# Three x tiles loaded early and transposed on TensorE instead of two, with K by chunk of wk and then Q tile by tile, in a gated mix of linear attention and a feed-forward block

## The chip, the cores and the metric

The kernel runs on one core of one Trainium2 chip. The metric is device time in microseconds (us). Before the change it is 274.4 us, the median of three runs (274.22 to 274.67). The record gives their granted TensorE clock as 1.0 over the whole span; that figure does not count a start at half rate. Names used below: PE is the TensorE matmul, PEld its weight load, DVE is VectorE, ACT is ScalarE, SP is SyncE. SP and ACT each issue DMAs into a queue of their own.

## The reference

Only the head of branch A matters here: x (2048 x 640) times the K, Q and V parts of `wqkv`, and a gate per row.

```python
def _A_ref(x, wqkv, wo):
    qkv = ...(x @ wqkv)...                       # H = 32 heads of 20
    phi = lambda t: jnp.where(t > 0, t + 1, jnp.exp(t)) + 1e-6
    pq, pk = phi(q), phi(k)
    ...                                          # linear attention, then @ wo
g = _sigmoid((x * gate_w).sum(-1, keepdims=True))
return g * a + (1 - g) * b                       # b: a GEGLU feed-forward block on x
```

## The kernel before

x is cut into 16 tiles of 128 rows, and its 640 columns into 5 chunks. For each tile the kernel computes K and Q (phi of both is kept). A matmul needs x transposed. Tiles 0 and 1 are loaded as they are and transposed on TensorE (`T`); tiles 2 to 15 are transposed by the DMA. K of tiles 0 and 1 runs chunk by chunk while the chunks of wk land. The gate's logit comes out of the Q matmul as a 129th column: `gate_col` transposes `gate_w` on PE into a column of wq.

The loads, in their order in the program (SP is the queue unless "act" is given):

```python
load touch ("act"); load_x(0); load_wk(0)
load_x(1, "act")
load_wk(1); load_wk(3)
... exp table load on ACT ...
load_wk(2, "act"); load_wk(4, "act")
P.op("dve", lambda e: e.memset(gw_sb, 0.0), writes=[r_gw])
dma_in(gw_sb[0:5, :], gate_w.rearrange("(k p) -> k p", p=128), [r_gw], eng="act")
load_wq(0, 2); load_wq(2, KC, "act")
for i in range(NXN, NT):                         # NXN = 2: DMA transposes on SP, after wk4
    load_xT(i, after=([r_wk[4]] if i == NXN else ()))
... x again for later, then the feed-forward weights ...
```

The order on PE. `KM(n, ks)` adds chunks `ks` into the K of item n, one matmul of 512 columns and one of 128 per chunk; `QM` does it for Q. An item n owns the pair of PSUM banks `SLOTS[n % 4]`. `phi1` is the exp on ACT, `phi2` two operations on DVE; only after them is the pair of banks free.

```python
seq = [("k", 0), ("k", 1), ("q", 0), ("q", 1)]
warm(5, 512); warm(1, 128)                       # matmuls of constants, to keep PE busy
T(0, [0], 7); T(0, [1, 2, 3, 4], 6); warm(6, 128)
KM(0, [0])
T(1, [0], 7); T(1, [1, 2, 3, 4], 6); warm(3, 128)
KM(1, [0])
for k in (1, 3): KM(0, [k]); KM(1, [k])
gate_col()
for k in (2, 4): KM(0, [k]); KM(1, [k])
for n in range(4):
    if n == 2: ...                               # Q of tiles 0 and 1, chunks interleaved
    phi1(n); phi2(n)
for i in range(2, NT):
    KQ(i)                                        # K and Q of a tile together, 15 matmuls
```

## Time and profile before

| | before |
|---|---|
| time, median of the first 3 runs | 274.4 us |
| span of the profiled run | 273.2 us, PE busy 269.7 us |
| first K matmul | 4.62 us |
| gate column | 7.56 us |
| first Q matmul | 8.67 us |
| tile 2 (first joint tile) starts | 11.40 us |

First the page of the kernel before: its span line, PE's busy time (us, share of the span, instructions), and the chain that ended last, by engine and by line.

```profile
span 273.2 us, 3449 instructions
PE 269.7 (99%) x1369; PEld 128.6 (47%) x1369; DVE 141.9 (52%) x251; ACT 76.0 (28%) x132; POOL 30.0 (11%) x28
...
PE 97%; DMA 2%; SPq 0%; DVE 0%; issue 0%
PE ps L701 41%; PE ps L865 23%; PE ps L540 14%; PE ps L597 6%; PE ps L844 4%; DMA pool<-in_A_wqkv_dram 2%; PE ps L679 2%; PE ps L812 2%; PE ps L600 1%; PE ps L468 1%; PE ps L825 1%; PE ps L453 1%; PE ps L722 1%; PE ps L740 0%; SPq L340 0%; PE ps L469 0%
```

PE makes up the chain but for 2% spent on one load of wqkv. Next, PE's waits in the first 60 us of the kernel before: who waited for whom, us in total, how often, the longest.

```profile
PE ps L419 <- PEq L915: 0.8, 1, 0.8
PE ps L453 <- DMA pool<-in_A_wqkv_dram: 0.8, 2, 0.6
```

So PE waits for the program to start, and twice for wk, and never again. The timeline of PE (start, duration, line, tiles, shape; what ended an idle time stands in brackets) shows where. L453 and L454 are the two matmuls of `KM`, L498 is the gate column, L468 begins Q, L540 is `KQ`.

```profile
6.20 0.22 PE L454 MATMUL ps<-pool 128*128 128x128 bf16 x1
7.01 0.39 PE L453 MATMUL ps<-pool 128*128 128x512 bf16 x1 [0.59 <-DMA pool<-in_A_wqkv_dram]
...
7.56 0.17 PE L498 MATMUL ps<-pool 128*128 128x5 bf16 x1
...
8.67 0.38 PE L468 MATMUL ps<-pool 128*128 128x512 bf16 x1
...
11.40 5.79 PE L540 MATMUL ps<-pool 128*128 128x512 bf16 x31
```

A matmul's drawn end lies behind its true occupation of PE, so starts are the better measure: a pair of 512 and 128 columns starts 0.27 us after the last one, and here 0.81 us pass between 6.20 and 7.01 where 0.06 would do. That is a hole of 0.75 us, ended by wk3. It is what the change goes after.

### The profile page before, as it was taken

What the parts mean: (1) busy time and instruction counts of PE and PEld (TensorE: products, weight loads), DVE (VectorE), ACT (ScalarE), POOL (GpSimd) and SP (SyncE); (2) the same over time, 40 slices, a digit from 0 to 9 for tenths busy, and PEclk for the clock granted to TensorE, in tenths of its full rate; (3) what the DMA queues carried; (4) which work ended last, traced back from release to release, by engine and by line L of the source; (5) the groups of instructions that cost most, each with busy time, mean ns of one, the idle gap of its engine ahead of it and who ended that gap; (6) DMA issues with size and microseconds to landing.
All of it is one profiled execution on the core that took longest, in us unless ns stands there. A gap on an engine that the chain in (4) does not pass through costs nothing.

```text
span 273.2 us, 3449 instructions
## 1 busy us (share of the span) xinstructions
PE 269.7 (99%) x1369; PEld 128.6 (47%) x1369; DVE 141.9 (52%) x251; ACT 76.0 (28%) x132; POOL 30.0 (11%) x28
## 2 busy tenths in 40 slices
PE   7999999999999999999999999999999999999997
PEld 4555555544445444444444444444444444444444
DVE  2588989998234334999999999634210000000200
ACT  2355555310421454223222223224011121121021
POOL 5000000003240001242332422000000000000000
PEclk9999999999999999999999999999999999999999
DMA  6675999500300011522121221263031110110211
GB/s 207 179 118 122 322 402 386 143 3 12 65 19 2 23 49 51 182 45 48 26 48 24 48 42 34 60 215 109 5 77 38 41 38 19 38 41 19 58 58 41
DMA packets 42160, 23.61 MB, mean 86 GB/s; under 512 B 31519, under 2 KB 40735, under 8 KB 42015
## 3 DMA queue, kind: packets, MB, share of 16 engines
q1 hardware_dynamic: 41269, 22.40, 30.0%
q10 hardware_dynamic: 874, 0.98, 1.0%
q8 instruction: 11, 0.18, 0.3%
q14 instruction: 6, 0.05, 0.0%
HBM read 13.83 MB, written 2.63 MB: 60 GB/s over the span
## 4 chain that ended last, share of the span: by engine, by line
PE 97%; DMA 2%; SPq 0%; DVE 0%; issue 0%
PE ps L701 41%; PE ps L865 23%; PE ps L540 14%; PE ps L597 6%; PE ps L844 4%; DMA pool<-in_A_wqkv_dram 2%; PE ps L679 2%; PE ps L812 2%; PE ps L600 1%; PE ps L468 1%; PE ps L825 1%; PE ps L453 1%; PE ps L722 1%; PE ps L740 0%; SPq L340 0%; PE ps L469 0%
## 5 line engine op out<-in xcount | busy, mean ns | idle before, releaser
L701 PE MATMUL ps<-pool 128*128 128x512 bf16 x520 | 113.7, 379 | 0.0
L701 PEld LDWEIGHTS ps<-pool 128*128 128x128 bf16 x520 | 50.5, 98 | 60.0
L865 PE MATMUL ps<-pool 128*128 128x512 bf16 (+2 forms) x306 | 62.7, 367 | 0.0
L707 ACT ACTIVATE pool<-ps 128x512 f32<-128x512 f32 x52 | 31.0, 597 | 73.1 <-PE ps L701 73.1
L709 DVE TENSOR_TENSOR pool<-ps,pool 128x512 bf16<-128x512 f32 x52 | 34.7, 689 | 31.7 <-PE ps L701 30.4
L865 PEld LDWEIGHTS ps<-pool 128*128 128x128 bf16 x306 | 29.2, 98 | 33.4 <-issue 0.4
L540 PE MATMUL ps<-pool 128*128 128x512 bf16 (+1 forms) x210 | 38.1, 344 | 0.0
L848 DVE TENSOR_TENSOR pool<-ps,pool 128x512 bf16<-128x512 f32 x4 | 2.8, 692 | 61.5 <-PE ps L844 61.5
L755 POOL TENSOR_TENSOR pool<-pool 128x640 f32<-128x640 bf16 x16 | 22.5, 1406 | 72.9 <-DVE pool L757 66.2
L872 ACT ACTIVATE pool<-ps,pool 128x512 bf16<-128x512 f32 (+1 forms) x16 | 10.9, 681 | 68.6 <-PE ps L865 68.6
L540 PEld LDWEIGHTS ps<-pool 128*128 128x128 bf16 x210 | 20.5, 98 | 17.5
L559 DVE SCALAR_TENSOR_TENSOR pool<-ps,pool 128x128 bf16<-128x128 f32 (+2 forms) x42 | 25.3, 602 | 2.4
L550 ACT ACTIVATE pool<-ps 128x640 bf16<-128x640 f32 x28 | 19.7, 704 | 18.2 <-DVE pool L559 10.9
L597 PE MATMUL ps<-pool 128*128 128x512 bf16 x78 | 19.4, 379 | 0.0
L765 DVE TENSOR_TENSOR pool<-pool 128x640 bf16<-128x640 bf16 x16 | 13.2, 826 | 0.6
L763 DVE TENSOR_SCALAR pool<-pool 128x32 f32<-128x32 f32 x16 | 12.8, 802 | 0.6
L757 DVE TENSOR_REDUCE pool<-pool 128x32 f32<-128x640 f32 x16 | 12.9, 807 | 0.0
L645 DVE TENSOR_TENSOR pool<-pool 128x640 f32<-128x640 f32 x14 | 11.6, 825 | 0.5
L844 PE MATMUL ps<-pool 128*128 128x512 bf16 x52 | 11.6, 379 | 0.0
L647 POOL PARTITION_ALL_REDUCE pool<-pool x1 | 4.0, 3972 | 61.5 <-DVE pool L645 61.5
L597 PEld LDWEIGHTS ps<-pool 128*128 128x128 bf16 x78 | 7.0, 98 | 7.3
L556 DVE TENSOR_SCALAR pool<-pool 128x640 bf16<-128x640 bf16 x28 | 9.2, 327 | 1.8 <-ACT pool L550 0.3
(70 smaller groups left out, 105.8 us busy)
## 6 DMA issues: line engine op xcount, KB each, us to landing
out_dram<-pool SPq DMA_DIRECT2D x19, 128.0 KB, 1.7
pool<-in_B_w_gate_dram SPq DMA_DIRECT2D x1, 2080.0 KB, 13.8
pool<-in_B_w_up_dram SPq DMA_DIRECT2D x1, 2080.0 KB, 19.3
pool<-in_A_x_dram SPq DMA_DIRECT2D x1, 1280.0 KB, 8.6
pool<-in_B_w_down_dram SPq DMA_DIRECT2D x1, 1120.0 KB, 6.0
pool<-omg_row SPq DMA_DIRECT2D x1, 1024.0 KB, 4.8
pool<-in_A_x_dram SPq DMA_DIRECT2D x1, 960.0 KB, 5.7
pool<-in_A_wo_dram SPq DMA_DIRECT2D x6, 160.0 KB, 10.0
```

The source lines that it names most:

```text
L540: last = e.matmul(ps[:, b + p, 0:c1 - c0], xT[:, k, i * 128:(i + 1) * 128], wkq[:, k, c0:c1], start=(k == 0), stop=(k == KC - 1))
L550: P.op("act", lambda e: e.activation(e_buf[m], ps_flat[:, o:o + 640], ACT.Exp), reads=banks, writes=[r_e[m]])
L559: P.op("dve", lambda e, c0=c0, c1=c1: e.scalar_tensor_tensor(dst[:, c0:c1], ps_flat[:, o + c0:o + c1], 1.0 + EPS, e_buf[m][:, c0:c1], ALU. ...
L597: last = e.matmul(ps[:, b, :], pk[i][:, c * 128:(c + 1) * 128], x_aug[:, i, 0:512], start=(i == 0), stop=(i == NT - 1))
L701: last = e.matmul(ps[:, b, :], w[:, k, fc * 128:(fc + 1) * 128], xT[:, k, j * 512:(j + 1) * 512], start=(k == 0), stop=(k == KC - 1))
L707: P.op("act", lambda e: e.activation(ge[n], ps[:, gb, :], ACT.Gelu_apprx_tanh), reads=[bank[gb]], writes=[r_ge[n]])
L709: P.op("dve", lambda e: e.tensor_tensor(hT[fc][:, j * 512:(j + 1) * 512], ps[:, ub, :], ge[n], ALU.mult), reads=[bank[ub], r_ge[n]], write ...
L755: P.op("pool", lambda e: e.tensor_tensor(tmp[n], pq[i], z_b, ALU.mult), reads=[r_pq[i], r_zb], writes=[r_tmp[n]])
L757: P.op("dve", lambda e: e.tensor_reduce(den[n], tmp[n].rearrange("p (h d) -> p h d", h=32), AX.X, ALU.add), reads=[r_tmp[n]], writes=[r_de ...
L765: P.op("dve", lambda e: e.tensor_tensor(pq[i].rearrange("p (h d) -> p h d", h=32), pq[i].rearrange("p (h d) -> p h d", h=32), den[n].unsqu ...
L844: last = e.matmul(ps[:, b, :], wd[:, fc, 512:640], hT[fc][:, j * 512:(j + 1) * 512], start=False, stop=(fc == NFC - 2), skip_group_check=True)
L865: last = e.matmul(ps[:, pb, 0:c1 - c0], lhs, rhs, start=False, stop=(q == len(rows) - 1), skip_group_check=True)
```

## The change

A third tile is loaded early on the ACT queue and transposed on PE, so that its K work fills the time in which PE waits for wk. Q of tiles 0 to 2 then follows tile by tile. The core of the diff:

```diff
-NXN = 2
+NXN = 3
             load_x(1, "act")
+            load_x(2, "act")
             load_wk(1)
 ...
-seq = [("k", 0), ("k", 1), ("q", 0), ("q", 1)]
+seq = [("k", 0), ("k", 1), ("k", 2), ("q", 0), ("q", 1), ("q", 2)]
 ...
             KM(1, [0])
-            for k in (1, 3):
-                KM(0, [k])
-                KM(1, [k])
+            KM(0, [1])
+            T(2, [0], 7)
+            T(2, [1, 2, 3, 4], 6)
+            KM(1, [1])
+            KM(2, [0])
+            KM(2, [1])
             gate_col()
-            for k in (2, 4):
-                KM(0, [k])
-                KM(1, [k])
-            for n in range(4):
-                (Q of tiles 0 and 1 interleaved by chunk at n == 2)
+            for k in (3, 2, 4):
+                for n in range(3):
+                    KM(n, [k])
+            for n in range(6):
+                if n == 3: QM(n, [0, 1]); QM(n, [2, 3, 4])
+                elif n > 3: QM(n, ALLK)
                 phi1(n)
                 phi2(n)
 ...
-                b = 3 * (i % 2)
+                b = 4 if i == 3 else 3 * (i % 2)
-            for i in range(2, NT):
+            for i in range(3, NT):
                 KQ(i)
```

The gate column now stands ahead of chunk 3, where before it stood behind it. And the load of tile 2 stands ahead of wk2, wk4 and `gate_w` on the ACT queue.

More of the change, by code (lines that the diff above doesn't have):

```diff
@@ L514, in bass_gated_mix__linear_attn_block__geglu_ffn__prompt_kernel @@
             KM(1, [0])
-            for k in (1, 3):
-                KM(0, [k])
-                KM(1, [k])
-            gate_col()
-            for k in (2, 4):
-                KM(0, [k])
-                KM(1, [k])
-            for n in range(4):
-                if n == 2:
-                    for k in range(3):
-                        QM(2, [k])
-                        QM(3, [k])
-                    QM(2, [3, 4])
-                    QM(3, [3, 4])
+            KM(0, [1])
[4 more added lines that the diff above has]
+            KM(2, [1])
+            gate_col()
+            for k in (3, 2, 4):
+                for n in range(3):
+                    KM(n, [k])
+            for n in range(6):
+                if n == 3:
+                    QM(n, [0, 1])
+                    QM(n, [2, 3, 4])
+                elif n > 3:
+                    QM(n, ALLK)
                 phi1(n)
```

## The prediction

> **What bounds the kernel.** TensorE. The page's first part has PE busy 269.7 of 273.2 us, and the chain of waits is 97% PE. From 7.0 us to the last output PE waits for nothing (waits of PE: 0.8 us for the start, 0.8 us for wk, no more), so only the first 14 us, up to the end of tile 2, can change the time. There the timeline shows: transposes of tile 0 at 3.17 us, first K matmul at 4.62 (wk0 landed), K of chunk 1 until about 6.25, idle until wk3 lands (K at 7.01), the gate column at 7.56, then no gap: Q from 8.67, tile 2 (K and Q as one) from 11.40 to 14.11. The granted clock is full from 4.2 us.
>
> **What the change does.** Tile 2 comes by a plain load and TensorE transposes instead of a DMA transpose. Added: five transposes (T(1) took 0.28 us on PE) and two DVE copies (0.23 and 0.42 us, hidden). The work of tile 2 is otherwise the same: 10 pairs of K or Q matmuls took 2.73 us, a joint tile 2.71. The intent is to fill the 0.75 us hole before wk3 with T(2) and K of tile 2 (0.28 + 0.55 us).
>
> **What I expect instead.** The 160 KB load of tile 2 is put on the ACT queue ahead of wk2, wk4 and gate_w. By the records of landings in the trace, the ACT queue now lands x1 at 4.68, wk2 5.68, wk4 7.15, gate_w 7.35; the SP queue wk1 5.46, wk3 6.96, wq0-1 8.53. The two queues advance side by side, about 1 us per 160 KB each. The Trainium skill ("DMA: Bandwidth & Descriptors", "Queues, rings and completion order") says that each engine consumes a queue's descriptors in order and round-robins between queues; gate_w landing 0.2 us behind wk4 agrees. So tile 2 takes wk2's place (about 5.7), wk2 wk4's (7.15), wk4 moves to about 8.2 to 8.5, and gate_w to about 8.4 to 8.7. But the change also moves the gate column, which needs gate_w, ahead of chunks 3, 2, 4. PE runs in order: it reaches the gate column at about 7.2 us and waits there 1.2 us, with wk3 and wk2 already landed. The hole is not filled but moved and widened.
>
> Then (g = 8.5 us): nine K pairs of 0.273 us until g + 2.5; q of tile 0 until g + 3.9; q of tile 1 needs banks 0 and 1, free when phi of the first K tile is done (2.4 us after its last chunk began, as at 8.13 to 10.52 now), so at g + 4.2: a stall of 0.3 us; tile 2 ends at g + 6.9 = 15.4 instead of 14.1. After it nothing waits, so all shifts: +1.0 to +1.3 us. wq and the later DMA transposes land in time.
>
> **Prediction: 275.5 us, 274.2 to 276.3 (8 in 10).** Faster by over 2%: 0.005; within 2%: 0.985; slower: 0.01.
>
> **What would show it.** PE waiting about 1.2 us on the gate_w load before the gate-column matmul; no wait for wk3; tile 2's load landing near 5.7 us and no wait of its transposes over 0.2 us; about 0.3 us of PE wait on DVE (phi) before q of tile 1; steady tiles still 2.71 us each; tile 3 starting near 15.4 us.
>
> **What would make it wrong.** If gate_w still lands near 7.35 us, K waits only for wk4 (about 8.3) and the result is 0.2 us better to 0.3 us worse. If tile 2's load slows wk0 or x1, which it follows on the queues, the start slips too, up to 0.5 us more. If phi of the K tiles is later released, the stall before q of tile 1 grows.

## The result, and the profile after

The changed kernel took 275.14 us (median of 6, 274.83 to 275.38), the kernel before 274.53 us beside it (median of 6, 274.22 to 274.78). The ratio is 1.0022, with a 95% interval of 1.001 to 1.0035. A ratio here is the mean time of one kernel's fast runs over that of the other's of the same rounds, so it is not quite the ratio of the medians. Later the same changed kernel gave 275.75 us (ratio 1.0043) and 275.24 us (1.0031). The loss is small and real: 0.6 to 1.3 us.

The page of the kernel after, same lines as before:

```profile
span 274.0 us, 3468 instructions
PE 270.8 (99%) x1379; PEld 129.3 (47%) x1379; DVE 142.2 (52%) x252; ACT 76.0 (28%) x132; POOL 29.9 (11%) x28
...
PE 97%; DMA 1%; DVE 1%; ACT 0%; issue 0%; SPq 0%
```

PE's waits in the first 60 us after:

```profile
PE ps L420 <- PEq L918: 0.8, 1, 0.8
PE ps L454 <- DMA pool<-in_A_wqkv_dram: 0.4, 1, 0.4
```

And its timeline (lines are one to three further down: L454 and L455 are `KM`, L434 is `T`, L499 is the gate column, L469 and L470 are `QM`, L543 is `KQ` of tile 3):

```profile
6.10 0.63 PE L454 MATMUL ps<-pool 128*128 128x512 bf16 x1
6.52 0.27 PE L455 MATMUL ps<-pool 128*128 128x128 bf16 x1
6.63 0.38 PE L454 MATMUL ps<-pool 128*128 128x512 bf16 x1
...
8.14 0.17 PE L499 MATMUL ps<-pool 128*128 128x5 bf16 x1
...
11.92 0.22 PE L470 MATMUL ps<-pool 128*128 128x129 bf16 x1
12.25 0.39 PE L469 MATMUL ps<-pool 128*128 128x512 bf16 x1
...
14.99 2.32 PE L543 MATMUL ps<-pool 128*128 128x512 bf16 x10
```

Three readings. First, tile 3 starts at 14.99 us. In the kernel before it started at 14.11 (11.40 plus one joint tile). That is 0.88 us, and the profiled run is 0.78 us longer (275.27 against 274.49). Second, there is a step of 0.33 us before Q of tile 1, at 12.25. The chain of waits passes through it: exp on ACT, then the two phi operations on DVE, then Q.

```profile
10.27 0.71 ACT pool L479
11.01 0.34 DVE pool L489
11.37 0.84 DVE pool L493
12.25 0.39 PE ps L469
```

Third, the predicted wait of 1.2 us at the gate column is not there. PE got to it at 8.14 us, just as `gate_w` had landed (8.04 us). PE was that late because its early matmuls were slow: the 512-column matmul at 6.10 took until 6.52, 0.42 us from start to start, and the one at 6.63 took 0.21 us. TensorE was at half rate until about 6.5 us. In the profile of before it was at full rate from 4.2 us. So one profile leaves it open which of the two delays counted. The experiments had to separate them.

### The profile page after: what moved, and what is told of

The parts are those of the page before. It is cut to its first block, busy times and chain, and to the rows that moved or that the text cites. A ratio compares the mean times of both kernels' runs of the same rounds, so it can differ in the third digit from the quotient of the medians.

```text
span 274.0 us, 3468 instructions
## 1 busy us (share of the span) xinstructions
PE 270.8 (99%) x1379; PEld 129.3 (47%) x1379; DVE 142.2 (52%) x252; ACT 76.0 (28%) x132; POOL 29.9 (11%) x28
## 4 chain that ended last, share of the span: by engine, by line
PE 97%; DMA 1%; DVE 1%; ACT 0%; issue 0%; SPq 0%
PE ps L704 41%; PE ps L868 23%; PE ps L543 13%; PE ps L600 6%; PE ps L847 4%; PE ps L815 2%; PE ps L682 2%; PE ps L603 1%; PE ps L454 1%; DMA pool<-in_A_wqkv_dram 1%; PE ps L469 1%; PE ps L828 1%; PE ps L725 1%; PE ps L743 0%; DVE pool L493 0%; PE ps L434 0%
## 5 line engine op out<-in xcount | busy, mean ns | idle before, releaser
L704 PEld LDWEIGHTS ps<-pool 128*128 128x128 bf16 x520 | 50.4, 98 | 60.1
L868 PEld LDWEIGHTS ps<-pool 128*128 128x128 bf16 x306 | 29.2, 98 | 33.4 <-issue 0.4
L543 PE MATMUL ps<-pool 128*128 128x512 bf16 (+1 forms) x195 | 35.4, 344 | 0.0
L543 PEld LDWEIGHTS ps<-pool 128*128 128x128 bf16 x195 | 19.0, 98 | 16.2
L562 DVE SCALAR_TENSOR_TENSOR pool<-ps,pool 128x128 bf16<-128x128 f32 (+2 forms) x39 | 23.5, 602 | 2.2
L553 ACT ACTIVATE pool<-ps 128x640 bf16<-128x640 f32 x26 | 18.3, 704 | 17.0 <-DVE pool L562 10.1
L600 PEld LDWEIGHTS ps<-pool 128*128 128x128 bf16 x78 | 7.0, 98 | 7.3
L559 DVE TENSOR_SCALAR pool<-pool 128x640 bf16<-128x640 bf16 x26 | 8.5, 327 | 1.6 <-ACT pool L553 0.2
```

The source lines that it names most:

```text
L543: last = e.matmul(ps[:, b + p, 0:c1 - c0], xT[:, k, i * 128:(i + 1) * 128], wkq[:, k, c0:c1], start=(k == 0), stop=(k == KC - 1))
L553: P.op("act", lambda e: e.activation(e_buf[m], ps_flat[:, o:o + 640], ACT.Exp), reads=banks, writes=[r_e[m]])
L562: P.op("dve", lambda e, c0=c0, c1=c1: e.scalar_tensor_tensor(dst[:, c0:c1], ps_flat[:, o + c0:o + c1], 1.0 + EPS, e_buf[m][:, c0:c1], ALU. ...
L600: last = e.matmul(ps[:, b, :], pk[i][:, c * 128:(c + 1) * 128], x_aug[:, i, 0:512], start=(i == 0), stop=(i == NT - 1))
L704: last = e.matmul(ps[:, b, :], w[:, k, fc * 128:(fc + 1) * 128], xT[:, k, j * 512:(j + 1) * 512], start=(k == 0), stop=(k == KC - 1))
L868: last = e.matmul(ps[:, pb, 0:c1 - c0], lhs, rhs, start=False, stop=(q == len(rows) - 1), skip_group_check=True)
```

## The experiments

Theory A: PE runs in order and stands at the gate column until `gate_w` lands behind the loads ahead of it. Theory B: the added transposes (0.28 us) and the wait on phi (0.33 us) make up the loss; they add to 0.61 us, which is just the first measured difference. Theory C: the late full clock made the difference, by chance.

Most runs were timed in 5 rounds beside the kernel before. In every profile of every kernel, the profiled time less the start of tile 3 is 260.28 to 260.38 us. (In eight profiles one early matmul record is missing, so the start of tile 3 was counted from the order of the program.) So whatever differs happens before tile 3, and its start can stand for the time. The table has what each profile showed, in us. "Half rate" is when the last matmul at half rate started. "Gate waits" is the time from start to start before the gate column less the 0.06 us that the matmul ahead of it takes. The landing of `gate_w` is read from the completion records of the trace.

| run | half rate until | gate_w lands | gate column | gate waits | tile 3 starts | profiled time | timed median | ratio to before |
|---|---|---|---|---|---|---|---|---|
| before | 4.1 | 7.35 | 7.56 | 0 | 14.11 | 274.49 | 274.53 | |
| after | 6.5 | 8.04 | 8.14 | 0 | 14.99 | 275.27 | 275.14 | 1.0022 |
| a_same | 6.6 | 8.36 | 8.41 | 0.44 | 15.26 | 275.55 | 275.75 | 1.0043 |
| a_same2 | 5.0 | 8.20 | 8.24 | 0.79 | 15.10 | 275.42 | 275.24 | 1.0031 |
| a_gw_early | 3.8 | 4.50 | 8.12 | 0 | 14.97 | 275.30 | 275.69 | 1.0040 |
| a_gate_late | 4.0 | 8.10 | 8.75 | 0 | 13.97 | 274.30 | 274.95 | 1.0012 |
| a_gw_sp | 3.9 | 6.67 | 6.96 | 0 | 13.80 | 274.13 | 274.30 | 1.0002 |
| a_gw_sp2 | 5.9 | 6.54 | 7.95 | 0 | 14.79 | 275.12 | 274.98 | 1.0011 |
| a_phi | 3.8 | 7.88 | 7.93 | 0.60 | 14.50 | 274.78 | 274.78 | 1.0013 |
| a_tilewise | 4.1 | 6.41 | 8.35 | 0 | 13.82 | 274.10 | 274.26 | 0.9997 |
| b_gw_last | 4.0 | 9.69 | 9.73 | 2.18 | 16.29 | 276.58 | 276.50 | 1.0084 |
| b_x2load | 3.7 | 7.87 | 7.92 | 1.00 | 14.50 | 274.88 | 275.16 | 1.0030 |
| b_x2load_gw_sp | 4.4 | 6.88 | 7.91 | 0 | 14.51 | 274.80 | 274.92 | 1.0016 |
| b_k2 | 3.6 | 6.53 | 7.41 | 0 | 13.80 | 274.12 | 274.35 | 0.9996 |

Names beginning with a are variants of the changed kernel, with b of the kernel before. The kernel before had medians of 274.44, 274.35 and 274.44 us (11 runs each).

### a_same and a_same2: the changed kernel again

No edit.

> The changed kernel again, unaltered. Theory A (PE reaches the gate column before gate_w has landed) and theory C (the moment when TensorE gets its full clock differs between executions: 4.2 us in the profile of before, about 6.5 us in that of after, which alone made the first K matmuls 0.5 us later) differ here. If this profile has the full clock near 4.2 us, A expects PE to stand at the gate column from about 7.2 us until gate_w lands near 8.1 us, and tile 2 to end near 15.0 us all the same; C expects tile 2 to end 0.5 us or more earlier, near 14.4 us. Time in both: 0.4 to 0.8 us over before.

> The changed kernel once more, as the yardstick of this call. 0.5 to 1.3 us over before in every execution, with no fast group: an execution with an early clock (4 us) is held at the gate column until gate_w lands at 8.0 to 8.4 us, one with a late clock (6.5 us) gets there only at about 8.1 us.

Measured: neither profile had its full clock at 4.2 us, so the first question was not answered as it was put (the profile of a_phi, below, answers it). But both showed PE standing at the gate column. The one with the clock at about 5 us shows it best. This is PE's timeline of a_same2:

```profile
7.39 0.22 PE L455 MATMUL ps<-pool 128*128 128x128 bf16 x1
8.24 0.18 PE L499 MATMUL ps<-pool 128*128 128x5 bf16 x1 [0.63 <-DMA pool<-in_gate_w_dram]
8.28 0.38 PE L454 MATMUL ps<-pool 128*128 128x512 bf16 x1
```

The bracket names the load. By starts it is 0.85 us where 0.06 would do. In the three profiles of this kernel the waits were 0 (clock at 6.5), 0.44 (6.6) and 0.79 us (5.0). The case at 6.6 waits because `gate_w` landed later in that run (8.36), and PE began K earlier (4.30 instead of 4.75). Tile 3 starts at 14.99, 15.26 and 15.10 us: the clock differs by 1.6 us, the outcome by 0.27 us, and it comes 6.90 to 6.95 us after the landing of `gate_w` (8.04, 8.36, 8.20). In the first of the three that is chance: there PE itself came last, 0.1 us after the landing. In the other two the clock decides how long PE waits at the gate column, but `gate_w` decides when it goes on. That speaks against C as the sole cause. All 16 timed runs of this kernel are at 274.83 us or more; there is no fast group.

### b_gw_last: the same small load moved back, in the kernel before

```diff
-            dma_in(gw_sb[0:5, :], ..., [r_gw], eng="act")      # with its memset
             load_wq(0, 2)
             load_wq(2, KC, "act")
+            dma_in(gw_sb[0:5, :], ..., [r_gw], eng="act")
```

> The kernel before, with its gate_w load issued last on the ACT queue, after wq2-4 (which landed at 9.39 us). Theory A: the queue's order decides when gate_w lands (about 9.6 us), PE stands at the gate column from 7.6 us till then, and the whole time grows by the same 1.9 to 2.1 us, to about 276.5 us. If small loads do not queue behind the large ones, gate_w lands before 7.5 us and the time is that of before.

Measured: `gate_w` (1.2 KB) landed at 9.69 us, 0.17 us after the 480 KB of wq ahead of it (9.52), though it was issued at 3.17 us. PE's timeline of b_gw_last:

```profile
9.73 0.18 PE L498 MATMUL ps<-pool 128*128 128x5 bf16 x1 [2.02 <-DMA pool<-in_gate_w_dram]
```

The median is 276.50 us, 2.06 us over before. The Trainium skill ("DMA: Bandwidth & Descriptors", "Queues, rings and completion order") says that on each DMA engine descriptors are consumed in ring order. This run agrees: a later place in the queue moved the landing from 7.35 to 9.69 us at the same size, and with the 2.18 us of waiting at the gate column the whole grew by 2.06. For whole loads the order does not hold strictly: in b_x2load, the next run, `gate_w` landed at 7.87 us, before the 160 KB of wk4 that stand ahead of it (8.47).

### b_x2load: the load alone

```diff
             load_x(1, "act")
+            load_x(2, "act")
 ...         # the later bulk load of x starts at tile 3; DMA transposes and PE as before
```

> The kernel before, with only the load of tile 2 added early on the ACT queue where the change puts it (nothing uses it early: no third set of transposes, PE order of before). Theory A: the load alone pushes gate_w from 7.35 to 8.0 to 8.4 us, PE waits for it at the gate column, which starts at 8.1 to 8.4 instead of 7.56, and the time grows by 0.5 to 0.8 us: the whole loss of the change without any of its added work. Theory B (added transposes and the wait on phi): no change, within 0.2 us of before.

Measured: the load alone brings the wait. PE's timeline of b_x2load:

```profile
6.86 0.22 PE L455 MATMUL ps<-pool 128*128 128x128 bf16 x1
7.92 0.18 PE L499 MATMUL ps<-pool 128*128 128x5 bf16 x1 [0.84 <-DMA pool<-in_gate_w_dram]
```

The median is 0.81 us over before, the ratio 1.0030 (1.0008 to 1.0052), a loss of the size of the whole change, without any added transpose and without the wait on phi. In the profile tile 3 starts 0.39 us later than in before: PE waits 1.00 us for `gate_w`, but wk3 landed early (6.32), which left a hole of 0.22 us instead of 0.75. Theory B as the sole cause is refuted.

### a_gw_early: gate_w ahead of tile 2's load (inconclusive)

```diff
             load_x(1, "act")
+            dma_in(gw_sb[0:5, :], ..., [r_gw], eng="act")      # with its memset
             load_x(2, "act")
```

> The changed kernel with the small gate_w load issued on the ACT queue ahead of tile 2's load instead of after wk4; order of PE unchanged. Theory A: gate_w lands before 5.5 us, no wait at the gate column; with the full clock at 4.2 us chunk 3 begins near 7.3 us, but wk4 (8.15 us) is no limit, so up to 0.85 us come back in such executions and nothing in those with a late clock: 0.3 to 0.8 us faster than the changed kernel, about the time of before. Theory B (the loss is the 0.28 us of added transposes plus the 0.33 us wait of q of tile 1 on phi, which add up to the measured 0.61 us): no difference from the changed kernel.

Measured: 275.69 us, against 275.75 for the changed kernel: no gain, as B expected. The profile shows that the test was spoilt. `gate_w` landed at 4.50 us, but its issue occupied the ACT queue for 0.57 us, tile 2's load was issued at 2.32 instead of 1.71 us, and it landed at 6.82 instead of 5.63 us. PE's timeline of a_gw_early:

```profile
5.86 0.22 PE L455 MATMUL ps<-pool 128*128 128x128 bf16 x1
6.87 0.45 PE L434 MATMUL ps<-pool 128*128 128x128 bf16 x5 [0.79 <-DMA pool<-in_A_x_dram]
```

The wait had moved from the gate column to the transposes of tile 2. A test that takes a load out of a queue must not put it in front of another that is needed.

### a_gate_late: the gate column later on PE

```diff
-            gate_col()
             for k in (3, 2, 4):
+                if k == 4:
+                    gate_col()
                 for n in range(3): KM(n, [k])
```

> The changed kernel with the gate column placed between chunks 2 and 4 on PE; loads unchanged. Theory A: PE reaches it 1.64 us later, after gate_w has landed; as the run with gate_w loaded early: 0.3 to 0.8 us faster than the changed kernel. Theory B: no difference.

Measured: 274.95 us, 0.80 us below the changed kernel (275.75). PE passed the gate column at 8.75 us without a wait. The timed runs fall into two groups, 274.21 and 274.30, and 274.86 to 275.19; the profiled run, whose clock came early, is the one at 274.30. The slower group lies below the changed kernel (275.31 to 275.85); against before, the interval of the ratio (0.9998 to 1.0026) includes no change.

### a_gw_sp and a_gw_sp2: gate_w on the SP queue

```diff
             load_wk(3)
+            dma_in(gw_sb[0:5, :], ..., [r_gw])                 # SP, with its memset
 ...
-            dma_in(gw_sb[0:5, :], ..., [r_gw], eng="act")
```

> The changed kernel with gate_w on the SP queue after wk3 (the run that put it ahead of tile 2's load held that load back by 0.6 us of issue and by a second wait, so it did not answer). Theory A: no wait at the gate column; where the full clock comes near 4.2 us, chunk 3 starts at 7.2 to 7.3 us instead of 8.1 to 8.4, and tile 2 ends near 14.1; where it comes near 6.5 us, tile 2 ends near 14.8. In the timed runs 0.3 to 0.9 us faster than the changed kernel, so 0 to 0.6 us over before. Theory B: as the changed kernel, 0.6 to 1.2 us over before.

> The changed kernel with gate_w on the SP queue after wk3, again, to see whether its two groups of times (four near 274.2, two near 275.3) come back. If the late clock is what makes the slower group, a profile with the clock near 6.5 us has a time near 275.3 and one near 4 us has 274.2. Median 0.5 to 1.2 us below the changed kernel of this call.

Measured: 274.30 us with before at 274.35 (ratio 1.0002, 0.9978 to 1.0025), and 274.98 with before at 274.44 and the changed kernel at 275.24. The second is only 0.26 us below the changed kernel, less than the 0.5 expected, and their runs overlap. The groups came back: 274.06 to 274.34 and 275.29 to 275.38 in the first, 274.35 and 274.36 and 274.86 to 275.24 in the second. One profile fell into each group. Their tile 3 starts differ by 0.99 us: 0.34 because wk0 landed later in one (4.12 and 4.47 us), 0.65 by the clock. PE's timeline of a_gw_sp, with the early clock:

```profile
5.06 0.39 PE L454 MATMUL ps<-pool 128*128 128x512 bf16 x1
5.29 0.22 PE L455 MATMUL ps<-pool 128*128 128x128 bf16 x1
...
6.96 0.17 PE L499 MATMUL ps<-pool 128*128 128x5 bf16 x1
```

And of a_gw_sp2, with the late clock:

```profile
5.94 0.60 PE L454 MATMUL ps<-pool 128*128 128x512 bf16 x1
6.37 0.23 PE L455 MATMUL ps<-pool 128*128 128x128 bf16 x1
...
7.95 0.17 PE L499 MATMUL ps<-pool 128*128 128x5 bf16 x1
```

From the first K matmul (4.26 and 4.60 us) to the gate column PE took 2.70 us in one and 3.35 in the other, with no wait for a load over 0.1 us in either. The late clock costs 0.65 us here. In the kernel before, the hole ahead of wk3 could take up part of it (its one profile has an early clock, so this is not shown), and in the changed kernel the wait for `gate_w` takes it up (a_same and a_same2); a kernel that waits for nothing shows it in full. The Trainium skill ("TensorE: Matmul & The Clock Gate", "Part 1: The HAM clock gate") says that the activity window is free-running and the warm-up therefore varies from run to run. These profiles agree: the last matmul at half rate began at 3.6 to 6.6 us in 14 profiles that all start PE at 0.8 us. That the slower timed runs without a profile had the late clock, or a late wk0, is inferred from these two.

### b_x2load_gw_sp: the load alone, gate_w out of its way

Both edits of b_x2load and a_gw_sp on the kernel before.

> The same, with gate_w issued on the SP queue right after wk3, so that it no longer stands behind tile 2's load. Theory A: gate_w lands within 0.3 us of wk3 (6.2 to 7.3 us), no wait over 0.1 us at the gate column; wk4, now near 8.15 us, is reached at about 8.1 us; time within 0.2 us of before. If instead bandwidth taken by the load is what costs (wk4 itself late, any order), the loss stays at 0.3 us or more.

Measured: 274.92 us, 0.57 over before, ratio 1.0016 (0.9995 to 1.0037). The expectation failed. There was no wait at the gate column, but wk3 landed at 7.31 us instead of 6.96, and PE waited 1.20 us for it by starts, where the hole of before was 0.75:

```profile
PE ps L454 <- DMA pool<-in_A_wqkv_dram: 1.0, 1, 1.0
```

That is the line of PE's waits of b_x2load_gw_sp. The early load may have held wk3 back, but that is not shown: with the same load in front, wk3 landed at 6.32 us in b_x2load and at 6.16 to 7.04 us in the changed kernel. The interval includes no change, and the median is only 0.24 us below that of b_x2load, so the timed runs do not tell how much of b_x2load's loss is `gate_w`; its profile does.

### b_k2: another way to fill the hole

```diff
-            for k in (1, 3): KM(0, [k]); KM(1, [k])
+            for k in (1, 2, 3): KM(0, [k]); KM(1, [k])
             gate_col()
-            for k in (2, 4): KM(0, [k]); KM(1, [k])
+            KM(0, [4]); KM(1, [4])
```

> Another way to fill the hole: the kernel before with K chunks in the order 1, 2, 3, gate, 4 instead of 1, 3, gate, 2, 4; loads unchanged. In the profile of before wk2 landed at 5.68 and wk3 at 6.96 us, so K of chunk 2 (0.55 us) fits into the hole of 0.75 us before chunk 3, and the Q part should start 0.3 to 0.55 us earlier (near 8.2 instead of 8.67): 274.0 us, 0.2 to 0.5 us below before. If wk2 and wk3 often land together, nothing is gained.

Measured: 274.35 us, as before; a miss. In its profile wk2 and wk3 landed at 5.62 and 6.07 us, so no hole was left to fill, and K ended early only to wait for wq. PE's waits of b_k2:

```profile
PE ps L453 <- DMA pool<-in_A_wqkv_dram: 0.5, 1, 0.5
PE ps L468 <- DMA pool<-in_A_wqkv_dram: 0.2, 1, 0.2
```

The second line is new: Q (L468) waits for wq. In the kernel before K ended later than wq0-1 landed (8.53 us), so this limit could not be seen.

### a_phi: K of tile 0 finished earlier

```diff
             gate_col()
-            for k in (3, 2, 4):
-                for n in range(3): KM(n, [k])
+            for n in range(3): KM(n, [3])
+            for n in range(3): KM(n, [2]); KM(n, [4])
```

> The changed kernel with the loads and the gate column untouched, but K of chunks 2 and 4 done tile by tile instead of chunk by chunk, so K of tile 0 ends two pairs (0.55 us) earlier. The wait of q of tile 1 on phi (0.33 us in all profiles of the changed kernel) should vanish, and the time fall by 0.3 us against the changed kernel of this call, whatever the gate column costs: the two terms add.

Measured: the step of 0.33 us before Q of tile 1 is gone. In the waits of PEld the changed kernel (a_same2) has

```profile
PEld ps L499 <- DMA pool<-in_gate_w_dram: 1.0, 1, 1.0
...
PEld ps L469 <- DVE pool L493: 0.4, 1, 0.4
```

and a_phi has only

```profile
PEld ps L499 <- DMA pool<-in_gate_w_dram: 0.8, 1, 0.8
```

From the gate column to tile 3 it takes 6.57 us instead of 6.86 in a_same2 (7.93 to 14.50, and 8.24 to 15.10). The profiled runs differ by 0.64 us, 0.29 of it here and 0.31 from `gate_w`, which happened to land earlier in the one of a_phi (7.88 instead of 8.20). The timed median is 0.46 us below the changed kernel; the part of that beyond 0.29 us is not accounted for run by run.

This profile also answers what a_same had asked, for everything up to the gate column is as in the changed kernel and the clock was early (half rate until 3.8 us). PE's timeline of a_phi:

```profile
7.28 0.22 PE L455 MATMUL ps<-pool 128*128 128x128 bf16 x1
7.93 0.18 PE L499 MATMUL ps<-pool 128*128 128x5 bf16 x1 [0.43 <-DMA pool<-in_gate_w_dram]
```

PE was ready for the gate column at 7.33 us, near the predicted 7.2, and stood there 0.60 us by starts. In the first profile, with its first K matmul at nearly the same time (4.75 and 4.72 us), the late clock brought PE there only at 8.14 us.

### a_tilewise: the mends together

The edits of a_gw_sp and a_phi, and the gate column behind chunk 2 of tile 0.

> All mends together: gate_w on the SP queue after wk3, gate column after chunk 2 of tile 0, K of chunks 2 and 4 tile by tile. Executions with an early clock: tile 2 ends near 13.45 us (14.11 in before), 273.7 to 273.9 us; with a late clock near 14.5 us, 274.6 to 275.0. Median 0.3 us below the kernel with gate_w on SP, 0.8 to 1.5 below the changed kernel, 0 to 0.7 below before.

Measured: 274.26 us, 0.98 us below the changed kernel, and level with before (274.44; ratio 0.9997, 0.9985 to 1.001). Tile 3 started at 13.82 us, not 13.45, mostly because K began at 4.58 us (wk0 landed at 4.45) and not at 4.26 as in a_gw_sp. From first K to tile 3 it took 9.24 us, against 9.49 in before. The view lists no wait of PE for a DMA in it; its waits of PE are this line alone:

```profile
PE ps L420 <- PEq L923: 0.8, 1, 0.8
```

## Why the prediction was right

The predicted time of 275.5 us was 1.1 us over before; measured were 0.61, 1.31 and 0.80 us over before, the first being the one compared. Point by point:

- **PE bounds the kernel and only the time before tile 3 can change.** Right: the remainder after the start of tile 3 is 260.28 to 260.38 us in all 14 profiles.
- **Tile 2's load takes wk2's place in the ACT queue.** Right: it landed at 5.63 to 5.78 us (predicted 5.7; wk2 had 5.68 before). wk4 landed at 7.94 to 8.15 us (predicted 8.2 to 8.5).
- **gate_w lands at 8.4 to 8.7 us and PE waits for it.** The mechanism was right, the size too large: it landed at 8.04, 8.36 and 8.20 us. This is the term that was mis-sized. It moved by 0.68 to 1.01 us, where 1.05 to 1.35 was predicted: wk4 came earlier than predicted, and `gate_w` landed between 0.10 us before it and 0.26 us after it, not always 0.2 after. The b_gw_last and b_x2load runs show the mechanism with nothing else changed.
- **PE waits 1.2 us at the gate column, from 7.2 us on.** Wrong in size, and not seen at all in the first profile: the waits were 0, 0.44 and 0.79 us. The step that failed is the assumption that PE always gets there at 7.2 us. That held for a clock that is full from 4.2 us, as in the profile of before. With a later clock PE comes later and the same landing is waited for less. In a_same and a_same2 the end was not changed by it, because there the end follows `gate_w`. In the compared profile `gate_w` cost nothing: a_gw_sp2, with `gate_w` out of the way and nearly as late a clock, takes 10.19 us from the first K matmul to tile 3, the compared profile 10.24, and the kernel before 9.49. That profile lost its time mostly to a late clock that no hole took up, which the prediction did not have, so that its number fits is partly luck.
- **A wait of 0.3 us before Q of tile 1.** Right: 0.33 us from start to start, 0.28 us after taking off what the matmul ahead of it needs, in every profile of the changed kernel, and gone in a_phi.
- **Tile 3 starts at g + 6.9 us, with g the gate column.** Right: 6.85, 6.85 and 6.86 us in the three profiles. With g mis-sized by 0.1 to 0.4 us, tile 3 started at 14.99 to 15.26 instead of 15.4.

Why does mending `gate_w` not make the change a gain? Counted from the first K matmul to tile 3, the terms for executions with an early clock are these, in us. Idle time is start to start less what the same shape takes back to back, and single gaps under 0.1 us are left out of the explained sum except the one after T(1).

| | before | a_gw_sp | a_tilewise |
|---|---|---|---|
| hole before wk3 | 0.75 | 0 | 0 |
| wait after T(1) | 0.09 | 0.09 | 0.09 |
| wait for the copy of T(2) | - | 0.14 | 0.14 |
| wait of Q of tile 1 on phi | - | 0.28 | 0 |
| transposes of tile 2 on PE | - | 0.28 | 0.28 |
| sum | 0.84 | 0.79 | 0.51 |
| first K to tile 3, measured | 9.49 | 9.54 | 9.24 |

The hole of 0.75 us was filled as intended. What fills it costs 0.70 us of its own in a_gw_sp: transposes that took no time of PE when the DMA did them, a copy that PE waits for, and a bank that is not free. Only without the wait on phi does the filled kernel come out ahead, by 0.25 us (the sums say 0.33), and the timed runs do not resolve that gain: the interval of a_tilewise includes 1, and the kernel that waits for nothing also takes a late clock in full. So no version here is shown to beat the kernel before.

What stays open: why wk3 and the loads near it land in some executions at 6.0 to 6.3 us and in others at 6.7 to 7.3 us, also with the same kernel (6.16, 7.04 and 6.67 us in three profiles of the changed one); the clock of runs without a profile; and whether the early load itself holds wk3 back (b_x2load_gw_sp).

## What to carry to other kernels

When a load is put into a queue, look at everything behind it there, the smallest loads above all, and at where an in-order engine needs each; a load of 1.2 KB whose user was moved forward while it moved back held PE for up to 0.79 us here. Before filling a hole, add up what the filling brings along (here 0.70 us for a hole of 0.75), and consider that a kernel without a hole in its start takes a late clock in full (0.65 us in a_gw_sp2). And where effects are below 1 us, one profile is one execution: read several of the same kernel before believing a wait, or its absence.

## What the Trainium skill lacked or had wrong

- "DMA: Bandwidth & Descriptors", "Issuing engines are not separate DMA queues", calls the sequencer's time to initiate a DMA "usually small relative to the DMA itself". Here the issue of the 1.2 KB `gate_w` in five rows took 0.57 to 0.64 us on the ACT queue (0.38 us on the SP queue), longer than that of 160 KB in 128 rows on the ACT queue (0.34 to 0.47 us), and putting it in front moved the next load's landing from 5.63 to 6.82 us. The page does not have the issue time of a load with few rows.
- "TensorE: Matmul & The Clock Gate", "Part 1: The HAM clock gate", says that the warm-up varies from run to run, as it does here, but its ±500 ns for the moment of the transition is too narrow: half rate lasted until 3.6 to 6.6 us in 14 profiles that start PE at the same time. It advises not to fit a cold count, since the penalty is under 1% of a typical span; here 0.65 us is 0.24% of the span and still as large as the effect under study. The page lacks the point that a kernel's early waits can hide this penalty (in a_same and a_same2 tile 3 came 6.90 us after `gate_w` with the clock at 6.6 and at 5.0 us), and that a kernel without them shows it.
- No page has the two groups of landing times of the early loads (wk3 at 6.0 to 6.3 or 6.7 to 7.3 us).
